# Attention with a threshold, then a feed-forward layer, on one core: preparation of the weights and of batch 0 laid out anew

## The chip, the core and the metric

The kernel runs on one core of a Trainium2 chip. A core has five engines that run side by side, each through its own queue in strict program order: TensorE (PE; its weight loads are listed as PEld), VectorE (DVE), ScalarE (ACT), GpSimd (POOL) and SyncE (SP, which here issues all transfers, run by 16 DMA engines). The metric is device time in microseconds (us) of one execution, compared by medians.

## The reference

```python
scores = (1 / sqrt(64)) * q @ k.T                    # 8 batches, 8 heads, 576 x 576
thresh = max(scores, axis=-1) - tau                  # tau = 0.02
scores = where(scores >= thresh, scores, -1e9)
attn = exp(scores - max(scores)); attn /= sum(attn) + 1e-9
x = (attn @ v), heads side by side                   # 4608 tokens x 512
h = x @ w_in                                         # 512 -> 2048
g = where(h >= 1, h, where(h <= -1, 0, (h + 1)**2 / 4))
out = g @ w_out                                      # 2048 -> 512, float32
```

q, k and v come in float32 with the head dimension first; w_in and w_out come in float64, as pairs of 32-bit words.

## The kernel before

**Precision.** Every large product is made of three float16 products: an operand is scaled by a power of two found from its own sums of squares and split into a float16 high part and a float16 low part (the remainder), and high x high, high x low and low x high are summed in PSUM.

**Weights (add_w, lines 424 to 541).** Each matrix is handled in 16 chunks of 128 x 512. A chunk of doubles is loaded to a staging place (SP, L449); ACT scales the high words to fix the exponent, in place (L457); DVE puts the float32 together in three bit passes, through a PSUM buffer `ph` (L463, L468, L472); PE squares it for the scale (L479). When all 16 chunks of a matrix are there the scale is known (lines 498 to 515), and each chunk is normalized on ACT (L522), rounded to its high part on ACT (L525), and its low part is the difference, on POOL (L528). w_in is staged in the eight places that w_out (`WO`) will need later; w_out is staged in two of the `x` buffers (`x3`, `x4`), so at most two of its chunks are under way.

**Queries, keys, values.** Two heads make a pair. add_qk loads a pair's q and k (L295), sums squares (L301, L309), makes scales on small `pc` tiles (L237 to L239 on DVE, L320 to L329 on POOL), normalizes (L337), splits (L340, L344) and copies by DMA into `qq` and `kk` (L355, L357). add_v does the same for v, and turns it by DMA transpose (L404, L409, L412).

**Attention.** The work comes in tiles of 128 queries of one head; j counts them, 288 in all (nine for each pair of a batch). A tile: four matmuls into one of two `s` buffers (L619), maximum on DVE (L630, L631, L632), exp on ACT (L635), mask and sum on DVE (L639, L643, L644), division on POOL (L647), high part on ACT (L650), low part on POOL (L653), DMA transpose into `eT` (L656). A batch's queries come in two parts, 256 of each of the four pairs and then 320; after each part PE multiplies by v (L693) into a `ph` buffer, and ACT and DVE write the two halves of `x` (L701, L705).

**Feed-forward.** A step takes 128 tokens and four chunks of 128 of the 2048: 48 matmuls (FFN1, L754) into `ph`, the gate on ACT and DVE (L760 to L775) into one of four `g` buffers, 12 matmuls (FFN2, L781) into the one `acc` bank. 144 steps. FFN1 needs all pairs of its tokens and the low parts of w_in; FFN2 the low parts of w_out.

**Order.** Nothing is scheduled by the compiler: class Plan (lines 40 to 148) walks through all operations with rough costs, and each engine takes the ready operation with the smallest key whose buffers are free; that fixes each queue's order. Keys are tile numbers. Feed-forward steps have their own key, `kf`: it starts `LEAD` = 8 tiles behind the tokens' last tile and rises by 2 for each step; FFN2 has `kf + 1`. There are three `ph` buffers, and they serve bit passes, statistics, attention x v and FFN1.

## Time and profile before

| | us |
|---|---|
| median of three runs | 1217.39 (1214.46 to 1219.19) |
| profiled execution, its own time | 1215.47 |
| its span, first to last instruction | 1213.2 |
| busy: PE, PEld | 1081.5, 788.4 |
| busy: DVE, ACT, POOL | 961.9, 885.1, 819.6 |
| DMA queue q1 | 74.7% of 16 engines' span |

The page has the span in 40 slices with a digit for the busy share of each engine in each slice; groups of instructions by line, with busy time, mean duration, and the idle time of the engine ahead of them; and other views give the same for a stretch of the span, or the instructions in order of time. A row of a timeline starts with its start and its length in us; `x12` means twelve instructions in one row. Means of short DVE instructions overlap with their neighbours, so that a sum of means is more than the busy time.

### The profile page before, as it was taken

How to read it: one execution, taken by the hardware profiler on the slowest of the kernel's cores; microseconds unless marked ns; L12 is line 12 of the kernel's file. 1: busy time of each engine (PE TensorE's matmuls, PEld its weight loads, DVE VectorE, ACT ScalarE, POOL GpSimd, SP SyncE). 2: the span in 40 equal slices, each digit the busy share in tenths (PEclk: the TensorE clock that was granted, in tenths of full speed). 3: DMA queues.
4: the chain of work that ended last, by engine and by line, in shares of the span. 5: the costliest groups of instructions: out<-in, count | busy, mean ns of one | idle time of the engine just before them, and what ended most of it. 6: DMA issues, size and time to landing. Idle time of an engine off the chain costs nothing.

```text
span 1213.2 us, 31983 instructions
## 1 busy us (share of the span) xinstructions
PE 1081.5 (89%) x11946; PEld 788.4 (65%) x11946; DVE 961.9 (79%) x2789; ACT 885.1 (73%) x1526; POOL 819.6 (68%) x939
## 2 busy tenths in 40 slices
PE   2334687999989999999999998999999999999998
...
DVE  6978987779877897788877898888877997887422
...
PEclk9956798999989999999999999999999999999999
...
GB/s 317 241 230 206 209 168 89 210 96 129 170 200 149 99 135 182 211 127 94 174 205 159 100 156 205 208 100 96 188 204 147 105 170 183 142 98 97 59 11 18
DMA packets 443818, 184.54 MB, mean 152 GB/s; under 512 B 406288, under 2 KB 414480, under 8 KB 443664
## 3 DMA queue, kind: packets, MB, share of 16 engines
q1 hardware_dynamic: 443664, 182.52, 74.7%
...
## 4 chain that ended last, share of the span: by engine, by line
PE 56%; DVE 19%; POOL 7%; ACT 7%; issue 5%; DMA 5%; SPq 1%; ACTq 0%; DVEq 0%; POOLq 0%
PE acc L781 22%; PE ph L754 21%; PE s L619 7%; PE ph L693 6%; DVE e L639 4%; DVE sm L630 4%; POOL hl L653 2%; POOL e L647 2%; DMA eT<-hl 2%; ACT e L635 1%; POOL nat L344 1%; DMA kk<-nat 1%; DVE ph L468 1%; DVE vb L409 1%; DVE ph L463 1%
## 5 line engine op out<-in xcount | busy, mean ns | idle before, releaser
L653 POOL TENSOR_TENSOR hl<-e,hl 128x576 f16<-128x576 f32 x288 | 368.0, 1283 | 98.8 <-ACT hl L650 96.4
L754 PE MATMUL ph<-x,WI 128*128 128x128 f16 x6912 | 409.3, 220 | 7.6 <-DVE x L705 4.6
L754 PEld LDWEIGHTS <-WI 128*128 128x128 f16 x6912 | 398.5, 98 | 22.1 <-issue 10.4
L781 PE MATMUL acc<-WO,g 128*128 128x512 f16 x1728 | 399.5, 382 | 4.6 <-DVE g L775 3.9
L647 POOL TENSOR_SCALAR e<-e,sm 128x576 f32<-128x576 f32 x288 | 218.7, 765 | 163.1 <-DVE sm L643 86.0
L781 PEld LDWEIGHTS <-g 128*128 128x128 f16 x1728 | 165.5, 98 | 195.3 <-DVE g L775 10.7
L635 ACT ACTIVATE e<-s,sm,pc 128x576 f32<-128x576 f32 x288 | 236.4, 828 | 69.7 <-DVE sm L631 56.9
L630 DVE TENSOR_REDUCE sm<-s 128x1 f32<-128x576 f32 x288 | 216.1, 751 | 65.5 <-PE s L619 62.3
L639 DVE SCALAR_TENSOR_TENSOR e<-s,sm,e 128x576 f32<-128x576 f32 x288 | 230.4, 813 | 30.4 <-ACT e L635 23.6
L650 ACT ACTIVATE hl<-e 128x576 f16<-128x576 f32 x288 | 194.7, 680 | 74.9 <-POOL e L647 68.6
L619 PE MATMUL s<-kk,qq 128*128 128x288 f16 (+1 forms) x1280 | 187.7, 298 | 51.2 <-DVE e L639 45.1
L619 PEld LDWEIGHTS <-qq 128*128 128x128 f16 (+1 forms) x1280 | 111.4, 103 | 103.2 <-issue 69.0
L767 DVE SCALAR_TENSOR_TENSOR ph<-ph,scs,asq 128x512 f32<-128x512 f32 (+1 forms) x160 | 111.6, 700 | 62.0 <-ACT asq L763 60.3
L760 ACT ACTIVATE asq<-ph,scs 128x512 f32<-128x512 f32 (+1 forms) x160 | 115.3, 731 | 51.5 <-PE ph L754 50.7
L693 PE MATMUL ph<-eT,vst 128*64 128x256 f16 (+1 forms) x1792 | 127.8, 295 | 8.2 <-DVE g L775 4.0
L775 DVE SCALAR_TENSOR_TENSOR g<-ph,scs,g 128x512 f16<-128x512 f32 (+1 forms) x160 | 109.0, 689 | 28.6 <-ACT g L771 28.2
L693 PEld LDWEIGHTS <-vst 128*64 128x64 f16 x1792 | 100.9, 113 | 32.5 <-issue 17.5
L771 ACT ACTIVATE g<-ph,scs 128x512 f16<-128x512 f32 (+1 forms) x160 | 100.8, 641 | 28.5 <-DVE ph L767 26.5
L763 ACT ACTIVATE asq<-asq 128x512 f32<-128x512 f32 x144 | 90.4, 628 | 1.7
L344 POOL TENSOR_TENSOR nat<-raw,nat 128x576 f16<-128x576 f32 x64 | 81.6, 1280 | 8.7 <-ACT nat L340 8.2
L631 DVE TENSOR_SCALAR sm<-sm,pc 128x1 f32<-128x1 f32 x288 | 61.7, 214 | 10.4
L340 ACT ACTIVATE nat<-raw 128x576 f16<-128x576 f32 x64 | 43.2, 679 | 34.5 <-POOL raw L337 27.2
...
## 6 DMA issues: line engine op xcount, KB each, us to landing
kk<-nat SPq DMA_DIRECT2D x128, 144.0 KB, 3.1
...
qq<-nat SPq DMA_DIRECT2D x128, 72.0 KB, 2.3
...
```

The source lines that it names most:

```text
L619: T.matmul(ap(s, s_ps)[r, f, :SH], q[:, hd, c : c + n], k[:, hd, l, f * SH : (f + 1) * SH], start=l == 0, stop=l == 1)
L630: V.tensor_reduce(t[:, 0:1], sv(), AX.XY, ALU.max, negate=True)
L635: A.activation(halves(ap(e, es)), sv(), AF.Exp, bias=ap(m, sm)[:, 1:2], scale=ap(cb, pc)[:, 24 + v, 0:1])
L639: V.scalar_tensor_tensor(halves(ap(e, es)), sv(), t[:, 2:3], halves(ap(e, es)), ALU.is_ge, ALU.mult, accum_out=t[:, 3:4])
L647: G.tensor_scalar(ap(e, es), ap(e, es), ap(m, sm)[:, 5:6], 1.0, ALU.mult, ALU.mult)
L650: A.activation(ap(x, hl)[:, :S], ap(e, es), AF.Copy)
L653: G.tensor_tensor(ap(x, hl)[:, S:], ap(e, es), ap(x, hl)[:, :S], ALU.subtract)
L693: T.matmul(o[hd * D : (hd + 1) * D, :n], vt[:, k, hd * D : (hd + 1) * D], t[:, kb, hd * n : (hd + 1) * n], start=k == 0, stop=k == NVB - 1)
L754: T.matmul(h[:, i], WTh["i"][:, u, wl * 512 + c * P : wl * 512 + (c + 1) * P], x[:, cc, xl, c0 : c0 + P], start=m == 0, stop=m == 3 * NCC - 1)
L760: A.activation(tv()[:, :, c], hv()[:, :, c], AF.Relu, bias=scs[:, b, 2:3], scale=scs[:, b, 1:2])
L767: V.scalar_tensor_tensor(hv()[:, :, c], hv()[:, :, c], scs[:, b, 0:1], tv()[:, :, c], ALU.max, ALU.min)
L781: T.matmul(ap(ab, accs), gv()[:, i, gl], WTh["o"][:, fc + i, wl * 512 : (wl + 1) * 512], start=fc + i == 0 and m == 0, stop=fc + i == NFC ...
```

## The change

- **Weights' bit passes.** DVE's first pass (L463) goes. ACT, in place of the exponent fix, converts the low words to their top bits straight into `ph` (new line 530); the fix moves to POOL (line 523); DVE keeps two passes (535, 539).
- **Weights' low parts.** For all 16 chunks of w_in and every other chunk of w_out, POOL makes the high part with the scale in one instruction (606), PE makes the low part in PSUM: a float32 matmul with a diagonal of the scale, minus the high part (609, 610), and ACT writes it to float16 (613). The other eight chunks of w_out go as before.
- **Staging of w_out.** Nine places in place of two: four `x` buffers, the output buffer, and four places of `WO` that are free by then. Only `x0` is open for attention's results until w_out is in.
- **Batch 0.** Its queries come in parts of 128, 128 and 320, so that the first eight tiles are 128 queries of all heads. FFN1 of 128 tokens waits only for those tokens. These eight tiles skip POOL, and the DMA: PE turns and divides them by a float32 matmul with a diagonal (757), ACT and DVE write the two parts (766, 769). v of batch 0 is turned on PE the same way (469, 472, 476). The rest of batch 0 has 10 blocks to turn where there were 9, and 15 products with v where there were 14.
- **Scales.** The `pc` scale passes write PSUM where they wrote strided SBUF, with a copy more (line 349).
- **Keys.** matmuls of a tile get the key j - 12, attention x v its key - 6, `LEAD` is 14 (4 for the first group), the step 1.8, FFN2 `kf + 6`; preparation has new keys.

```diff
+WOFF = 2
+NPT = 8
+KQ, KV = (-5.9, -2.7, 0.5, 3.7), -2.1
+KI, KO = (-5.8, 0.73), (8.6, 0.3)
+QKP, AVP = 12, 6
+LEAD0, LEAD = 4, 14
+KF, F2 = 1.8, 6
...
-            def b1(stage=stage, pb=pb):
+            def low(stage=stage, pb=pb):
                 if F64:
-                    V.tensor_scalar(ap(pb, ph).bitcast(U32), stage()[:, :, 1], 3, None, ALU.logical_shift_left)
+                    A.activation(ap(pb, ph).bitcast(U32), stage()[:, :, 0], AF.Copy, scale=0.935 * 2.0 ** -29)
...
-                    V.scalar_tensor_tensor(t, stage()[:, :, 0], 29, t, ALU.logical_shift_right, ALU.bitwise_or)
+                    V.scalar_tensor_tensor(t, stage()[:, :, 1], 3, t, ALU.logical_shift_left, ALU.bitwise_or)
...
-                    A.activation(t, t, AF.Copy, scale=2.0 ** -112)
+                    G.tensor_scalar(t, t, 2.0 ** -112, 1.0, ALU.mult, ALU.mult)
...
+            def split(src=src, hi=hi):
+                G.tensor_scalar(hi, src, s[:, 0:1], 1.0, ALU.mult, ALU.mult)
+            def diff(src=src, hi=hi, lb=lb):
+                T.matmul(ap(lb, ph), dgw[w], src, start=True, stop=False)
+                T.matmul(ap(lb, ph), minus, hi, start=False, stop=True)
+            def rest(lo=lo, lb=lb):
+                A.activation(lo, ap(lb, ph), AF.Copy)
...
+        d_op = plan.op("POOL", 0.25, j, lambda: G.tensor_scalar(ap(d, dge), ident, ap(m, sm)[:, 5:6], 1.0, ALU.mult, ALU.mult), [o, c_op], take=[d], uses=[m])
+        for k0, k1 in ((0, 4), (4, 5)):
...
+                    T.matmul(ap(tb, ph)[:, (k - k0) * P : (k - k0 + 1) * P], ap(e, es)[:, k * P : (k + 1) * P], ap(d, dge), start=True, stop=True)
...
-        o = chained("qk", plan.op("PE", 0.5 if len(heads) == 1 else 0.7, j, qk, ready, take=[s], uses=[qb, kb], behind=prev.get("qk")))
+        o = chained("qk", plan.op("PE", 0.5 if len(heads) == 1 else 0.7, j - QKP, qk, ready, take=[s], uses=[qb, kb], behind=prev.get("qk")))
...
-            o = chained("f2", plan.op("PE", 12 * 0.216, kf + 1.0, ffn2, [o] + wo, take=[ab] if fc == 0 else [], uses=[qb, ab], behind=prev.get("f2")))
+            o = chained("f2", plan.op("PE", 12 * 0.216, kf + F2, ffn2, [o] + wo, take=[ab] if fc == 0 else [], uses=[qb, ab], behind=prev.get("f2")))
-            kf += 2.0
+            kf += KF
```

What this makes of the queues, at three places. On DVE, in the kernel before, around the last chunks of w_in (`ph` is the PSUM buffer that a chunk is put together in, `WO` the staging place, `sm` and `e` belong to a tile):

```order
L472 SCALAR_TENSOR_TENSOR WI_67<-WO_68,ph1_64 128x512
L463 TENSOR_SCALAR ph2_65<-WO_68 128x512
L463 TENSOR_SCALAR ph0_63<-WO_68 128x512
L468 SCALAR_TENSOR_TENSOR ph2_65<-WO_68,ph2_65 128x512
L237 TENSOR_SCALAR pc1_114<-ph1_64 128x6
L238 TENSOR_SCALAR pc1_114<-pc1_114 128x6
L239 TENSOR_SCALAR pc1_114<-pc1_114 128x6
L639 SCALAR_TENSOR_TENSOR e2_93,sm2_121<-s0_61,sm2_121,e2_93 128x576
L472 SCALAR_TENSOR_TENSOR WI_67<-WO_68,ph2_65 128x512
```

and in the changed kernel, around the last three chunks of w_in:

```order
L769 TENSOR_TENSOR eT1_99<-ph0_63,eT1_99 128x128
L535 SCALAR_TENSOR_TENSOR ph2_65<-WO_68,ph2_65 128x512
L717 TENSOR_SCALAR sm4_122<-sm4_122 128x1
L718 RECIPROCAL sm4_122<-sm4_122 128x1
L539 SCALAR_TENSOR_TENSOR WI_67<-WO_68,ph2_65 128x512
L535 SCALAR_TENSOR_TENSOR ph1_64<-WO_68,ph1_64 128x512
L713 SCALAR_TENSOR_TENSOR e1_92,sm5_123<-s1_62,sm5_123,e1_92 128x576
L809 SCALAR_TENSOR_TENSOR x0_103<-ph0_63,x0_103 128x128
L539 SCALAR_TENSOR_TENSOR WI_67<-WO_68,ph1_64 128x512
```

A chunk has two rows where it had three, and what is between them are rows of a tile that is turned on PE (L769 writes the low part of `eT`) and already a row of x (L809).

Where w_in's parts are made: on ACT, in the kernel before, right after its scale (`wsc_i`) is known:

```order
L522 ACTIVATE WI_67<-WI_67,wsc_i_135 128x512 x2
L525 ACTIVATE WI_67<-WI_67 128x512 x2
L301 ACTIVATE junk_127,pc3_116<-raw6_75 128x576
L522 ACTIVATE WI_67<-WI_67,wsc_i_135 128x512
L301 ACTIVATE junk_127,pc3_116<-raw0_69 128x576
L635 ACTIVATE e0_91<-s0_61,sm0_119,pc2_115 128x576
L525 ACTIVATE WI_67<-WI_67 128x512
```

and on POOL, in the changed kernel, at the same point:

```order
L585 TENSOR_SCALAR dgw_i_130<-ident_128,wsc_i_141 128x128
L606 TENSOR_SCALAR WI_67<-WI_67,wsc_i_141 128x512 x2
L750 TENSOR_SCALAR dge1_134<-ident_128,sm7_125 128x128
L523 TENSOR_SCALAR WO_68<-WO_68 128x512 x2
L606 TENSOR_SCALAR WI_67<-WI_67,wsc_i_141 128x512
L523 TENSOR_SCALAR WO_68<-WO_68 128x512
L721 TENSOR_SCALAR e0_91<-e0_91,sm0_118 128x576
L606 TENSOR_SCALAR WI_67<-WI_67,wsc_i_141 128x512
```

The two rows on ACT became one on POOL (L606), which shares its queue with the exponent fixes of w_out (L523) and the first tiles' divisions (L721).

On PE, in the changed kernel, the place where FFN1 first stands (`dgw` is the diagonal of the scale, `vst` v turned, `x0` the first 256 tokens' x):

```order
L797 MATMUL ph2_65<-eT0_98,vst2_89 64x128
L609 MATMUL ph0_63<-WI_67,dgw_i_130 128x512
L610 LDWEIGHTS minus_129
L610 MATMUL ph0_63<-WI_67,minus_129 128x512
L864 LDWEIGHTS WI_67
L864 MATMUL ph1_64<-x0_103,WI_67 128x128
```

The 16th and last difference of w_in (L609, L610) stands right ahead of the first FFN1 (L864). Up to that row PE has 80 matmuls of tiles (L693), where the kernel before has 92; up to the end of the eighth FFN2 both have 176.

More of the change, by code (lines that the diff above doesn't have):

```diff
@@ L7 @@
 from concourse._compat import with_exitstack
+from concourse.masks import make_identity
 F16 = mybir.dt.float16
@@ L266, in attn_ffn_kernel @@
     for b in range(B):
-        parts += [(b, p, h) for h in range(2) for p in range(NPAIR)]
+        parts += [(b, p, q0, n) for q0, n in (CUT0 if not b else CUT) for p in range(NPAIR)]
     tiles = []
     first, last = {}, {}
-    for i, (b, p, h) in enumerate(parts):
+    for i, (b, p, q0, n) in enumerate(parts):
         first[i] = len(tiles)
-        n, q0 = (S1, S0) if h else (S0, 0)
         r = n % P
@@ L280, in attn_ffn_kernel @@
     NS = len(tiles)
-    start = {x: first[i] for i, x in enumerate(parts)}
-    pidx = {x: i for i, x in enumerate(parts)}
+    start = {}
+    for i, (b, p, q0, n) in enumerate(parts):
+        start.setdefault((b, p), first[i])
     QK = {}
@@ L479, in gram @@
                     T.matmul(ap(gbuf, accs)[:, :P], c, c, start=u == 0 and x == 0, stop=u == NU - 1 and x == 3)
-            before = []
-            if w == "o":
-                before = [wbits["i", x] for x in range(NU) if x % (NFC // 2) == (u + 2) // 2]
-            l = plan.op("SP", 0.6, key - 5, load, before, take=[sb], work=1.75)
-            o1 = plan.op("ACT", 0.6, key - 1, fix, [l], uses=[sb])
-            o2 = plan.op("DVE", 0.55, key, b1, [o1] + before, take=[pb], uses=[sb])
-            o3 = plan.op("DVE", 0.62, key, b2, [o2], uses=[sb, pb])
-            o4 = wbits[w, u] = plan.op("DVE", 0.62, key, b3, [o3], uses=[sb, pb], behind=wbits.get((w, u - 1)))
+            mine = (at, at + 1) if isinstance(at, int) else (at,)
+            before = [x for n in mine for x in staged.get(n, [])]
+            over = list(staged.get(u + WOFF, [])) if w == "o" else []
+            l = plan.op("SP", 0.6, key - 5, load, before, work=1.75)
+            o1 = plan.op("POOL", 0.75, key - 1, fix, [l])
+            o2 = plan.op("ACT", 0.6, key, low, [l], take=[pb])
+            o3 = plan.op("DVE", 0.62, key, b2, [o1, o2], uses=[pb])
+            o4 = wbits[w, u] = plan.op("DVE", 0.62, key, b3, [o3] + over, uses=[pb], behind=wbits.get((w, u - 1)))
+            for n in mine:
+                staged[n] = [o4]
+            if w == "o" and u in XGIVE:
+                o4.gives = ("x", XGIVE[u])
             if not u:
@@ L532, in add_w @@
-                wlo[w, u] = plan.op("POOL", 1.15, key2, rest, [o])
-            else:
-                def split(src=src, hi=hi):
-                    A.activation(hi, src, AF.Copy, scale=s[:, 0:1])
-                def rest(src=src, hi=hi, lo=lo):
-                    V.scalar_tensor_tensor(lo, src, s[:, 0:1], hi, ALU.mult, ALU.subtract)
-                o = plan.op("ACT", 0.65, key2, split, before)
-                wlo[w, u] = plan.op("DVE", 0.9, key2, rest, [o])
+                o = plan.op("ACT", 0.57, key2, norm, [so])
@@ L543, in attn_ffn_kernel @@
+            def rest(lo=lo, lb=lb):
+                A.activation(lo, ap(lb, ph), AF.Copy)
+            o = plan.op("POOL", 0.75, key2, split, [wdf.get((w, u - WOFF)), so])
+            o = wdf[w, u] = plan.op("PE", 1.1, key2, diff, [o, dg], take=[lb])
+            wlo[w, u] = plan.op("ACT", 0.52, key2, rest, [o], uses=[lb])
     wbits = {}
-    def w_pool(w, u):
-        return True
     for b in range(B):
         for p in range(NPAIR):
-            t0 = start[b, p, 0]
-            add_qk(b, p, t0 if (b, p) != (0, 0) else -20)
-        add_v(b, start[b, 0, 0] + (0 if b else 4))
@@ L662, in add_tile @@
         o = plan.op("DVE", 0.26, j, sden, [o], uses=[m])
-        o = chained("norm", plan.op("POOL", 0.77, j, snorm, [o], uses=[e, m], behind=prev.get("norm")))
-        o = chained("hi", plan.op("ACT", 0.58, j, shi, [o], take=[x], uses=[e], behind=prev.get("hi")))
-        o = plan.op("POOL", 1.26, j, slo, [o], uses=[e, x])
-        o = chained("tr", plan.op("SP", 1.3, j, send, [o], take=[eTb[i]] if j == first[i] else [], uses=[x, eTb[i]], work=1.7, behind=prev.get("tr")))
-        part_tr[i].append(o)
+        take = [eTb[i]] if j == first[i] else []
```

221 lines of the change are left out of this document (149 added, 72 removed).

## The prediction

> **What bounds the kernel now.** I read the page's slices first: where is PE, the engine with the most work, not full?
>
> ```profile
> PE   2334687999989999999999998999999999999998
> DVE  6978987779877897788877898888877997887422
> PEclk9956798999989999999999999999999999999999
> ```
>
> PE is full from about the eighth slice (30.3 us each) to the end. Ahead of that it is a third to two thirds busy, DVE is at 7 to 9 tenths, and PE's granted clock is down to about half in slices 3 to 5. So there are two stages: a preparation that PE doesn't set, and a long stage that PE does. For where the one ends I took PE's timeline:
>
> ```profile
> 10.24 0.61 PE L479 MATMUL acc<-WI 128*128 128x128 bf16 x4 [3.45 <-DVE WI L472]
> 130.38 0.40 PE L479 MATMUL acc<-WO 128*128 128x128 bf16 x4
> 132.54 2.84 PE L754 MATMUL ph<-x,WI 128*128 128x128 f16 x48 [1.71 <-DVE x L705]
> 177.41 2.75 PE L781 MATMUL acc<-WO,g 128*128 128x512 f16 x12
> 200.13 4.95 PE L781 MATMUL acc<-WO,g 128*128 128x512 f16 x12
> 211.13 2.09 PE L693 MATMUL ph<-eT,vst 128*64 128x320 f16 x28
> 213.15 5.35 PE L781 MATMUL acc<-WO,g 128*128 128x512 f16 x24
> ```
>
> FFN1 starts at 132.5, FFN2 at 177.4, and the eighth FFN2 ends at 213.15 + 5.35 = 218.5. That last point is my milestone, since at the end of the eighth FFN2 both orders have done 176 matmuls of tiles and eight FFN1; the changed one is one product with v (2.09 us) short. Whatever the change gains up to there is kept if PE stays full behind it. A step costs PE 2.84 and 2.75 where the clock is full, and an FFN2 4.95 where it isn't; four matmuls of 128 columns took 0.61 early and 0.40 later, the same difference. Then the windows, cut at first FFN1 and at the milestone (us busy of PE, PEld, DVE, ACT, POOL; clock; DMA share; GB/s):
>
> ```profile
> 0.00:132.50 132.50, 49.73 (x337) 30.96 (x338) 109.38 (x293) 88.07 (x159) 88.81 (x117) 0.77 0.99 250
> 132.50:218.50 86.00, 69.68 (x701) 50.13 (x701) 68.16 (x193) 68.30 (x122) 74.64 (x81) 0.90 0.76 144
> 218.50:1213.20 994.70, 962.11 (x10911) 707.29 (x10908) 784.37 (x2304) 728.69 (x1247) 656.13 (x743) 0.99 0.72 140
> ```
>
> Up to 218.5 the sums are PE 119.4, DVE 177.5, ACT 156.4, POOL 163.5, and DMA 0.99 x 132.5 + 0.76 x 86 = 196.5. DVE, with 0.81 of the time, is the most loaded engine; the DMA engines are as loaded, but part of what they carry is the next batch, which nobody waits for yet. Behind the milestone PE idles 994.7 - 962.1 = 32.6 us.
>
> **The change, part by part.** First the preparation; the rows that price it:
>
> ```profile
> L463 DVE TENSOR_SCALAR ph<-x 128x512 uint32<-128x512 uint32 x16 | 11.1, 691 | 5.4 <-ACT x L457 5.3
> L457 ACT ACTIVATE x<-x 128x512 f32<-128x512 f32 x16 | 10.6, 661 | 3.1 <-DMA x<-in_moe_w_out_dram 3.0
> L522 ACT ACTIVATE WO<-WO,wsc_o 128x512 f32<-128x512 f32 x16 | 11.0, 721 | 0.0
> L525 ACT ACTIVATE WO<-WO 128x512 f16<-128x512 f32 x16 | 9.5, 629 | 0.0
> L528 POOL TENSOR_TENSOR WO<-WO 128x512 f16<-128x512 f32 x16 | 18.3, 1158 | 1.2 <-ACT WO L525 1.2
> L647 POOL TENSOR_SCALAR e<-e,sm 128x576 f32<-128x576 f32 x288 | 218.7, 765 | 163.1 <-DVE sm L643 86.0 <-DVE sm L644 70.5 <-DVE pc L237 5.6
> L653 POOL TENSOR_TENSOR hl<-e,hl 128x576 f16<-128x576 f32 x288 | 368.0, 1283 | 98.8 <-ACT hl L650 96.4
> L650 ACT ACTIVATE hl<-e 128x576 f16<-128x576 f32 x288 | 194.7, 680 | 74.9 <-POOL e L647 68.6 <-DMA eT<-hl 5.4
> L404 POOL TENSOR_SCALAR vb<-raw,scs 128x1152 f16<-128x1152 f32 x32 | 39.2, 1225 | 15.0 <-DVE scs L396 14.3 <-DVE sm L643 0.4 <-DMA vst<-vb 0.2
> L409 DVE SCALAR_TENSOR_TENSOR vb<-raw,scs,vb 128x576 f16<-128x576 f32 x32 | 37.2, 1161 | 5.3 <-POOL vb L404 5.3
> ```
>
> ```profile
> L771 ACT ACTIVATE g<-ph,scs 128x512 f16<-128x512 f32 x128 | 87.4, 684 | 25.0 <-DVE ph L767 23.1 <-PE acc L781 0.9
> L775 DVE SCALAR_TENSOR_TENSOR g<-ph,scs,g 128x512 f16<-128x512 f32 x128 | 95.1, 743 | 23.8 <-ACT g L771 23.3
> L705 DVE SCALAR_TENSOR_TENSOR x<-ph,x 128x256 f16<-128x256 f32 x64 | 26.6, 416 | 8.8 <-ACT x L701 8.7
> ```
>
> *DVE.* The first bit pass goes: 32 x 0.691 = -22.1. Four subtractions for v go (4 x 1.161 = -4.6). Twelve turned pieces (four of v, eight tiles) each need a subtraction of 512 columns from PSUM, 0.743 as L775, and one of 128, for which I take 0.28 (between 0.214 for 64 columns on the same line and L705's 0.416 for 256; the trace has no 128): +12.3. x in eight parts of 128 for four of 256: +0.6. Sum -13.8: 163.7.
>
> *POOL.* 24 of 32 subtractions go: 24 x 1.158 = -27.8. The first eight tiles skip POOL: 8 x (0.765 + 1.283) = -16.4; v of batch 0: 4 x 1.225 = -4.9. Added: 32 exponent fixes and 24 scaled high parts, each at L647's rate for 512 columns, 0.765 x 512/576 = 0.68: +38.1 (the trace has neither on POOL; the bounds are 0.54 by L404, 1.06 ns a column, and 1.14 by L653: +30 to +64). Eleven diagonals and 17 clears at about 0.2: +5. Sum -6: 157.5 (150 to 184).
>
> *ACT.* 24 normalizations and high parts go: 24 x (0.721 + 0.629) = -32.4. The exponent fix (0.661) becomes the conversion of low words, of the same size, at the same price; it hides where the fix hid. 24 low parts come from PSUM at L771's 0.684: +16.4. Eight high parts of tiles go (8 x 0.680 = -5.4), twelve turned pieces come (0.684 + 0.28): +11.6, x +0.6. Sum -9.2: 147.2.
>
> *PE.* New are 60 turned blocks of 128 columns and 24 differences of 512, all float32 but the second half of each difference. No row shows float32 on PE. Lower end, as float16 at full clock (2.84/48 = 0.059, 2.75/12 = 0.229): 60 x 0.059 + 48 x 0.229 = 14.5. Upper end: this kernel itself cuts an operand into two pieces, two by two make four products; four at the slow rows (0.61/4, 4.95/12): 60 x 0.61 + 24 x 5 x 0.413 = 86. I take four products at the full clock, 60 x 0.236 + 24 x 5 x 0.229 = 42, because they fill gaps that now let the clock fall. PE: 161 (134 to 205). The Trainium skill (FP8 and Floating Point Precision, TensorE Precision Notes) gives true float32 four passes through the array; by it the sum is the 42 where the clock is full and the 86 where it isn't.
>
> *DMA.* Twelve transposes leave the front of SP's queue and the DMA engines; the other 20 of batch 0 have 10 blocks for 9.
>
> ```profile
> q1 hardware_dynamic: 443664, 182.52, 74.7%
> ```
>
> That is 906 us for 182.5 MB; eight tiles of 0.295 MB and four v of 0.459 are 4.2 MB, -21, and the longer ones +3: about 179 is left. Every row behind them on SP, loads of w_out among them, is issued earlier by as much. Loads of w_out no longer wait for two places, so POOL and DVE can take up w_out while w_in is split.
>
> So up to the milestone the most loaded are DMA 179, DVE 164, PE 161, POOL 158. It was DVE with 0.81. Now four are near each other, and a chunk goes through POOL, PE and ACT in turn, which costs share; against it DVE, which everything else stood behind, is relieved. I take 0.83 for DVE: milestone at 198, 20.5 us earlier. Bounds: 0.90 (182), and 0.75, which POOL had (218, no gain). First FFN1, by DVE's work ahead of it (21 bit passes of two instructions for 29 of three, 16 tiles for 21, so some 73 us at 0.7): 104.
>
> Then the long stage. Who PE waited for there (us, times, longest):
>
> ```profile
> PE s L619 <- DVE e L639: 10.8, 13, 4.2
> PE ph L693 <- DVE g L775: 4.0, 4, 2.3
> PE acc L781 <- DVE g L775: 3.9, 7, 1.3
> PE ph L693 <- DVE pc L237: 2.7, 1, 2.7
> ```
>
> The waits of FFN2 for g (3.9) go: with `kf + 6` and steps of 1.8 two or three other steps lie between. Of the waits for DVE's mask (10.8) and for `ph` buffers (4.0, 2.7) I take half off, since tiles are ordered up to 12 ahead and DVE is relieved by the scale passes:
>
> ```profile
> L238 DVE TENSOR_SCALAR pc<-pc 128x6 uint32<-128x6 uint32 x32 | 17.5, 545 | 1.1
> L239 DVE TENSOR_SCALAR pc<-pc 128x6 uint32<-128x6 uint32 x32 | 17.1, 534 | 1.1
> L238 DVE TENSOR_SCALAR scs<-scs 128x1 uint32<-128x1 uint32 x8 | 1.2, 154 | 0.3
> ```
>
> Two passes at 0.54 become three that I price by the 0.154 of the same pass on `scs`: 0.62 for each of 32 pairs, 20 us of DVE, 2.5 a batch, none of it on PE. Together -11 (0 to -27, all that was waited for; below, a wait more, is the last rival). FFN1's and FFN2's own work is unchanged and hides nothing new.
>
> Sum: 1213.2 - 20.5 + 2.1 (the product with v) - 11 = 1183.8; with 2.3 around the span 1186; the median stood 1.9 above the profiled execution, so **1188**.
>
> **The rivals.** *PE sets the preparation.* All float32 at the upper end: 205 us on PE, at 0.93 the milestone is at 220, and 1213.2 + 1.5 + 2.1 - 11 + 4.2 = 1210. For it: bursts before ran at half speed. Against it: the clock was 0.99 wherever PE was full. The Trainium skill (TensorE: Matmul & The Clock Gate, Part 1) has the clock at half after an idle window of some 3.4 us and full after a busy one; by that rule the added work keeps it up and this rival fails. The row of the first window, 0.77 with PE busy 0.38 of it, agrees in direction.
>
> *The start is gained and lost again on `ph`.* Three buffers now serve bit passes (from ACT's conversion on, earlier than before), turned pieces and differences too. The waits of attention x v for `ph` above show the ring short already. If it holds shares to 0.75, the milestone stays at 218 and the steady gain is used up by batch 0's extra products: 1217.
>
> *All of it works better:* milestone at 182, all waits gone: 1213.2 - 36.5 + 2.1 - 27 + 4.2 = 1156.
>
> *Slower: tiles ahead of steps make PE stand.* PE's queue is strict, and a tile's first matmul waits for DVE's mask two tiles before. Before, 13 of some 276 did, 10.8 us in all. With keys 12 ahead each tile stands in front of a step that could run. At 0.17 us a tile on the mean, 47 us, it gives 1188 + 47 = 1235; slower than no change from 0.13 on, (1223.5 - 1188)/276. Against it: tiles stand singly between steps of 2.8 us, so there are 5 us between two of one buffer.
>
> **The numbers.** Less than 0.5% (6 us) can't be told from no change here. Forecast (1168 to 1204) 0.61; better 0.13; PE sets the start 0.10; lost again 0.08; slower 0.08. The range, 1160 to 1211, leaves out half of the better case and most of the last two. Faster: 0.61 + 0.13 + 0.06 (half or so of the case at 1210) = 0.80; same 0.04 + 0.08 = 0.12; slower 0.08.
>
> **What would show it.** First FFN1 near 104 and the eighth FFN2's end near 198 in PE's timeline; DVE some 14 us less up to there; a float32 difference of 1.1 us for both halves (0.46 and 2.1 are the ends); a clock over 0.77 in the first 100 us; PE's idle time behind the milestone near 22 us. I am wrong if PE is full ahead of the first FFN1, if `ph` releases the longest waits there, or if tiles' matmuls wait more than 11 us in the long stage.

## The result, and the profile of the changed kernel

The changed kernel takes 1170.91 us (median of four runs, 1169.09 to 1174.35), the one before 1215.93 (1214.04 to 1219.19, four runs): the ratio is 0.963, with a 95% interval of 0.9595 to 0.9666, that is 45 us less. The profiled execution took 1169.14 us, its span is 1167.4. The forecast was 1188 in a range of 1160 to 1211: direction and range were right, the gain was some 17 us larger than forecast.

The slices of the changed kernel's page, each now 29.2 us:

```profile
PE   4687889999999999999999999999999999999998
DVE  5899888889888998889888888888778998884232
PEclk9799899999999999999999999999999999999999
```

In slices 2 to 5 PE is 6 to 8 tenths busy, where it was 3 to 6, and it is full from the seventh slice on. The clock's digits 5, 6 and 7 of the old slices 3 to 5 have become 9, 9 and 8; slice 2 shows a 7 where it had a 9. PE's timeline of the changed kernel, with a few rows of the new float32 work (each float32 matmul is recorded as two MATMUL, so `x8` is four blocks) and the milestones:

```profile
14.36 2.08 PE L469 MATMUL ph<-dgv,raw 128*128 128x128 f32 x8 [1.48 <-POOL dgv L460]
24.81 1.16 PE L469 MATMUL ph<-dgv,raw 128*128 128x128 f32 x8 [0.97 <-DVE vst L476]
102.08 1.02 PE L609 MATMUL ph<-WI,dgw_i 128*128 128x512 f32 x2
102.94 0.38 PE L610 MATMUL ph<-WI,minus 128*128 128x512 f16 x1
106.00 1.13 PE L609 MATMUL ph<-WI,dgw_i 128*128 128x512 f32 x2
106.96 0.38 PE L610 MATMUL ph<-WI,minus 128*128 128x512 f16 x1
107.64 2.84 PE L864 MATMUL ph<-x,WI 128*128 128x128 f16 x48 [0.30 <-DVE WO L539]
140.03 2.75 PE L891 MATMUL acc<-WO,g 128*128 128x512 f16 x12
187.79 5.34 PE L891 MATMUL acc<-WO,g 128*128 128x512 f16 x24
```

FFN1 starts at 107.6 (132.5 before), FFN2 at 140.0 (177.4), and the eighth FFN2 ends at 187.79 + 5.34 = 193.1 (218.5).

The clock shown for the first microseconds is too high, in both kernels. Four float32 blocks take 2.08 us at 14.36 and 1.16 at 24.81, and the profile grants 1.00 in both places; the rows run at half speed up to 20.4. In the kernel before it shows 1.00 for the first 52 us, too, and its rows there are slow: four matmuls of a tile take 1.12, as in the row below, and 0.65 in the changed kernel at 127.43.

```profile
51.60 1.12 PE L619 MATMUL s<-kk,qq 128*128 128x288 f16 x4 [0.35 <-DVE e L639]
```

With half the clock in these stretches the mean ahead of the first FFN1 would be some 0.57 in the kernel before, where the profile has 0.77, and some 0.80 in the changed one, where it has 0.90 (estimates from these rows).

The windows cut at the first and the last of these (columns as in the prediction):

```profile
0.00:107.60 107.60, 71.96 (x579) 49.99 (x580) 88.14 (x261) 74.96 (x152) 78.20 (x147) 0.90 0.86 261
107.60:193.10 85.50, 75.31 (x754) 52.05 (x754) 73.50 (x215) 66.56 (x116) 73.26 (x87) 0.96 0.72 139
193.10:1167.40 974.30, 957.73 (x10944) 705.07 (x10941) 777.92 (x2339) 731.57 (x1255) 660.12 (x751) 1.00 0.76 145
```

Up to the milestone the kernel is 25.4 us shorter; behind it 20.4 us, in spite of one product with v more. There PE idles 974.3 - 957.7 = 16.6 us where it idled 32.6, and is busy 957.7 where it was 962.1. Whom PE waits for behind the milestone, by lines (the rows end with the idle time ahead of the instructions and its releasers), first in the kernel before:

```profile
L754 PE MATMUL ph<-x,WI 128*128 128x128 f16 x6528 | 382.5, 219 | 2.8 <-DVE x L705 1.5 <-DVE g L775 0.9 <-DVE pc L237 0.4
L781 PE MATMUL acc<-WO,g 128*128 128x512 f16 x1633 | 376.0, 381 | 4.4 <-DVE g L775 3.9 <-ACT g L771 0.3
L619 PE MATMUL s<-kk,qq 128*128 128x288 f16 (+1 forms) x1104 | 152.7, 288 | 11.1 <-DVE e L639 10.8
L693 PE MATMUL ph<-eT,vst 128*64 128x256 f16 (+1 forms) x1568 | 108.5, 290 | 8.2 <-DVE g L775 4.0 <-DVE pc L237 2.7 <-DVE scs L394 0.8
```

and in the changed kernel:

```profile
L864 PE MATMUL ph<-x,WI 128*128 128x128 f16 x6528 | 385.5, 219 | 2.1 <-DVE x L809 1.2 <-DVE g L885 0.8
L891 PE MATMUL acc<-WO,g 128*128 128x512 f16 x1633 | 373.7, 379 | 0.0
L693 PE MATMUL s<-kk,qq 128*128 128x288 f16 (+1 forms) x1104 | 155.9, 287 | 7.9 <-DVE e L713 5.2 <-DMA kk<-nat 2.5
L797 PE MATMUL ph<-eT,vst 128*64 128x320 f16 (+1 forms) x1598 | 108.9, 287 | 1.4 <-DMA eT<-hl 1.4
```

Products with v waited 8.2 us and now 1.4, FFN2 4.4 and now nothing, tiles 11.1 and now 7.9, 5.2 of it for the mask (L713).

### The profile page after: what moved, and what is told of

The parts are those of the page before. It is cut to its first block, busy times and chain, and to the rows that moved or that the text cites. A ratio compares the mean times of both kernels' runs of the same rounds, so it can differ in the third digit from the quotient of the medians.

```text
span 1167.4 us, 32610 instructions
## 1 busy us (share of the span) xinstructions
PE 1105.0 (95%) x12274; PEld 807.1 (69%) x12274; DVE 939.6 (80%) x2813; ACT 873.1 (75%) x1522; POOL 811.6 (70%) x983
## 3 DMA queue, kind: packets, MB, share of 16 engines
q1 hardware_dynamic: 430480, 179.24, 75.7%
## 4 chain that ended last, share of the span: by engine, by line
PE 64%; DVE 12%; POOL 8%; DMA 5%; issue 5%; ACT 4%; SPq 1%; POOLq 0%; ACTq 0%; DVEq 0%
PE ph L864 25%; PE acc L891 23%; PE s L693 8%; PE ph L797 7%; DVE sm L704 3%; DMA eT<-hl 2%; DVE e L713 2%; POOL hl L729 2%; POOL e L721 1%; POOL nat L378 1%; DMA kk<-nat 1%; DMA WO<-in_moe_w_in_dram 1%; POOL raw L371 1%; ACT hl L726 1%; DVE ph L877 1%
## 5 line engine op out<-in xcount | busy, mean ns | idle before, releaser
L729 POOL TENSOR_TENSOR hl<-e,hl 128x576 f16<-128x576 f32 x280 | 359.8, 1290 | 100.3 <-ACT hl L726 98.2
L864 PE MATMUL ph<-x,WI 128*128 128x128 f16 x6912 | 409.8, 219 | 5.1 <-DVE g L885 3.6
L864 PEld LDWEIGHTS <-WI 128*128 128x128 f16 x6912 | 396.3, 98 | 21.0 <-issue 8.6
L891 PE MATMUL acc<-WO,g 128*128 128x512 f16 x1728 | 395.0, 379 | 0.0
L721 POOL TENSOR_SCALAR e<-e,sm 128x576 f32<-128x576 f32 x280 | 212.9, 764 | 99.5 <-DVE sm L718 68.0
L713 DVE SCALAR_TENSOR_TENSOR e<-s,sm,e 128x576 f32<-128x576 f32 x288 | 231.9, 812 | 34.2 <-ACT e L709 31.0
L726 ACT ACTIVATE hl<-e 128x576 f16<-128x576 f32 x280 | 189.8, 679 | 70.2 <-POOL e L721 46.9
L693 PE MATMUL s<-kk,qq 128*128 128x288 f16 (+1 forms) x1280 | 182.5, 289 | 12.8 <-DVE e L713 9.9
L693 PEld LDWEIGHTS <-qq 128*128 128x128 f16 (+1 forms) x1280 | 106.5, 100 | 69.1 <-issue 31.7
L885 DVE SCALAR_TENSOR_TENSOR g<-ph,scs,g 128x512 f16<-128x512 f32 (+1 forms) x160 | 109.1, 691 | 27.0 <-ACT g L881 26.8
L797 PE MATMUL ph<-eT,vst 128*64 128x320 f16 (+2 forms) x1928 | 126.1, 283 | 4.3 <-DVE eT L769 2.8
L705 DVE TENSOR_SCALAR sm<-sm,pc 128x1 f32<-128x1 f32 x288 | 61.7, 214 | 10.2
L706 DVE TENSOR_SCALAR sm<-sm,pc 128x1 f32<-128x1 f32 x288 | 58.8, 204 | 0.0
```

Source lines behind the costliest of these rows:

```text
L693: T.matmul(ap(s, s_ps)[r, f, :SH], q[:, hd, c : c + n], k[:, hd, l, f * SH : (f + 1) * SH], start=l == 0, stop=l == 1)
L713: V.scalar_tensor_tensor(halves(ap(e, es)[:, :S]), sv(), t[:, 2:3], halves(ap(e, es)[:, :S]), ALU.is_ge, ALU.mult, accum_out=t[:, 3:4])
L721: G.tensor_scalar(ap(e, es)[:, :S], ap(e, es)[:, :S], ap(m, sm)[:, 5:6], 1.0, ALU.mult, ALU.mult)
L726: A.activation(ap(x, hl)[:, :S], ap(e, es)[:, :S], AF.Copy)
L729: G.tensor_tensor(ap(x, hl)[:, w : w + S], ap(e, es)[:, :S], ap(x, hl)[:, :S], ALU.subtract)
L797: T.matmul(o[hd * D : (hd + 1) * D, :n], vt[:, k, hd * D : (hd + 1) * D], t[:, kb, hd * n : (hd + 1) * n], start=m == 0, stop=m == len(blo ...
```

## The experiments

Since a span is the time in which PE is busy and the time in which it isn't, one table holds all kernels (us; span, busy and idle from the profiled execution; the ratio to the kernel before, from timed runs on the same chip, with its 95% interval). "Idle behind" is PE's idle time behind the end of the eighth FFN2. That end itself can only be compared where as many tile matmuls precede it: 176 in the kernels marked *, 180 in three passes and two places, 172 with tiles off PE; in the others 124 to 200.

| kernel | time | ratio, interval | PE busy | PE idle | idle behind | end of eighth FFN2 |
|---|---|---|---|---|---|---|
| before | 1215.9 | 1 | 1081.5 | 131.7 | 32.6 | 218.5 * |
| changed | 1170.9 | 0.963, 0.9595 to 0.9666 | 1105.0 | 62.4 | 16.6 | 193.1 * |
| old keys | 1204.4 | 0.9912, 0.9879 to 0.9946 | 1120.3 | 85.6 | 40.5 | 191.5 |
| before, new keys | 1192.3 | 0.9805, 0.9776 to 0.9834 | 1075.6 | 114.8 | 16.3 | 225.0 |
| tiles not ahead | 1189.6 | 0.9787, 0.9751 to 0.9823 | 1112.7 | 72.4 | 29.4 | 182.2 |
| FFN2 near | 1194.9 | 0.9822, 0.9793 to 0.9852 | 1114.9 | 77.7 | 31.3 | 188.9 |
| tiles further ahead | 1187.2 | 0.9761, 0.9735 to 0.9787 | 1110.8 | 73.2 | 28.3 | 189.8 * |
| step 1.85 | 1166.9 | 0.9592, 0.9563 to 0.962 | 1107.5 | 58.3 | 12.5 | 195.2 * |
| old scales | 1177.4 | 0.9694, 0.9654 to 0.9734 | 1108.5 | 66.3 | 19.1 | 196.4 * |
| three passes | 1199.9 | 0.987, 0.9851 to 0.9889 | 1115.1 | 82.6 | 25.5 | 211.9 |
| low parts off PE | 1194.8 | 0.9826, 0.9808 to 0.9844 | 1094.3 | 97.8 | 34.5 | 177.6 |
| tiles off PE | 1183.7 | 0.9736, 0.9713 to 0.976 | 1102.0 | 83.4 | 30.6 | 187.0 |
| two places | 1184.3 | 0.9747, 0.9724 to 0.9769 | 1111.6 | 70.3 | 21.2 | 200.3 |
| difference twice | 1177.4 | 0.9682, 0.9657 to 0.9708 | 1120.0 | 55.4 | 15.3 | 203.3 * |

**Old keys.** The changed kernel with the keys of before for tiles, steps and FFN2; the preparation and its keys stay new.

```diff
-QKP, AVP = 12, 6
-LEAD0, LEAD = 4, 14
-KF, F2 = 1.8, 6
+QKP, AVP = 0, 0
+LEAD0, LEAD = 8, 8
+KF, F2 = 2.0, 1
```

> The changed kernel with the order's old keys (tiles' matmuls and attention x v at their own tile number, steps 8 tiles behind and 2 apart, FFN2 at kf + 1); preparation's new keys stay. Behind the eighth FFN2 the change gained 20.4 us: PE's idle time fell from 32.6 to 16.6, and 4.4 us of busy time went too. Theory A, the keys made it: PE's idle time there goes back to about 32, and the time to 1188 to 1194 (0.978 to 0.982 of the kernel before). Theory B, the scale passes made it, which take 20 us off DVE: the time stays within 4 us of 1171 (0.960 to 0.966). The eighth FFN2 ends near 193 in both.

**Before, new keys.** The other way round: the kernel before with `LEAD` 14, tiles' matmuls and products with v at j - 12 and its key - 6, the step 1.8 and FFN2 at `kf + 6`, in the five lines of its code that hold these numbers.

```diff
...
-            kf += 2.0
+            kf += KF
...
```

> The kernel before with only the new keys of the order (tiles 12 ahead, attention x v 6 ahead, steps 14 behind and 1.8 apart, FFN2 at kf + 6). Theory A, the keys make the gain of the long stage: 1194 to 1202 (0.983 to 0.989), PE's idle time behind the eighth FFN2 near 17 us. Theory B, the scale passes make it: 1212 to 1220 (0.997 to 1.003), idle near 32. First FFN1 stays at about 132 in both, as preparation is not touched.

Old keys took 1204.4, ten above the upper end of what I had expected; the new keys alone 1192.3, two below the lower end. Both say the same: the keys are worth more than my long stage gave them, 24 us on the old preparation (1216.6, the kernel before on that chip, to 1192.3) and 33 on the new (1204.4 to 1170.9). The preparation is worth 12 with old keys, 21 with new ones. The table tells the two apart: with new keys on the old preparation the first FFN1 stays at 132.6, but PE's idle time behind the milestone falls to 16.3, just what the changed kernel has; with old keys on the new preparation the first FFN1 is at 112.3, and 40.5 us are idle behind. So the start belongs to the preparation, and the long stage's idle time to the keys. The windows behind the milestone, of old keys and of the kernel before with new keys:

```profile
191.51:1205.90 1014.39, 973.87 (x11002) 713.60 (x11000) 801.91 (x2389) 749.52 (x1275) 678.77 (x778) 0.99 0.76 143
225.03:1190.40 965.37, 949.05 (x10810) 696.45 (x10807) 770.41 (x2268) 717.94 (x1230) 647.30 (x731) 1.00 0.74 142
```

On PE's whole span the preparation takes off 46 us of idle time (old keys) or 52 (new), the keys 17 (old preparation) or 23 (new). In busy time the preparation adds 39 or 29, and the keys take off 6 or 15. So each half is worth more beside the other one, by 6 us in idle and 9 in busy time of the profiled executions. In the medians it is 9 in all: the gain of the whole is 45, the two halves alone give 24 and 12. Where those 15 come from is seen in 100 us windows of old keys:

```profile
100.00:200.00 100.00, 85.78 (x820) 56.43 (x820) 68.28 (x217) 69.31 (x117) 68.17 (x80) 0.92 0.60 109
200.00:300.00 100.00, 89.19 (x1002) 65.37 (x999) 78.57 (x231) 72.39 (x124) 70.93 (x82) 0.93 0.83 156
300.00:400.00 100.00, 91.91 (x1022) 66.50 (x1020) 87.30 (x263) 79.40 (x138) 81.52 (x95) 0.97 0.96 181
```

and of the changed kernel:

```profile
100.00:200.00 100.00, 87.62 (x898) 60.56 (x899) 87.06 (x261) 78.58 (x139) 86.04 (x105) 0.97 0.76 146
200.00:300.00 100.00, 97.19 (x1166) 73.36 (x1164) 87.54 (x274) 83.03 (x142) 79.68 (x91) 1.00 0.91 174
300.00:400.00 100.00, 100.00 (x1166) 74.67 (x1165) 89.05 (x272) 81.61 (x145) 76.37 (x84) 1.00 0.90 168
```

With old keys the early start is not used: from 100 to 300 DVE is only 68 and 79% busy, PE stands an eighth of the time, and the granted clock there is 0.92 and 0.93, so that what PE does takes longer as well. Over the three windows old keys lose 8 + 7 + 3 = 18 us to the clock and the changed kernel 3; the difference is as large as the 15 us of busy time. That is where I see what the whole gains beyond its halves.

**Tiles not ahead.** Only the keys of tiles' matmuls and products with v go back.

```diff
-QKP, AVP = 12, 6
+QKP, AVP = 0, 0
```

> The changed kernel with tiles' matmuls and attention x v back at their own tile number; the steps' keys (14 behind, 1.8 apart, FFN2 at kf + 6) stay new. If it is the tiles ahead of the steps that keep DVE supplied, most of the keys' gain goes: 1180 to 1190 (0.971 to 0.979), and DVE waits for tiles' matmuls as long as before (54 us behind the eighth FFN2, 36 in the changed kernel). If it is the steps' lag and FFN2's distance: 1169 to 1176 (0.961 to 0.967).

It took 1189.6, within the first range: in this order 19 us hang on the tiles being ahead. PE's waits for the mask behind the eighth FFN2 rose from 5.2 to 18.8 us (us in total, times, longest):

```profile
PE s L693 <- DVE e L713: 18.8, 13, 3.6
```

The other sign that I expected, DVE waiting for tiles' matmuls as long as before, was not there (22.6 us; 36.1 in the changed kernel, 54.4 before): DVE starves less in the long stage, and more at the hand-over, where it is busy 45.8 of the 74.7 us between the first FFN1 and the eighth FFN2.

**FFN2 near.** Only FFN2 goes back to one key behind its step.

```diff
-KF, F2 = 1.8, 6
+KF, F2 = 1.8, 1
```

> The changed kernel with FFN2 one key behind its step, as before, in place of six; steps, tiles and preparation stay. Theory A (my forecast: FFN2's distance is worth only the waits for g that it removes, 3.9 us): 1173 to 1178, and FFN2 waits for g some 4 us. Theory B (the distance is a good part of the long stage's gain, since one step less in between also keeps tiles from their turn): 1180 to 1192.

It took 1194.9, above even the second range. Taken out alone, this one number loses 24 us, and I had given it 3.9. PE's waits behind the eighth FFN2 in this kernel (us in total, times, longest):

```profile
PE s L693 <- DVE e L713: 14.7, 9, 5.4
PE ph L864 <- DVE pc L349: 5.8, 2, 3.2
PE acc L891 <- DVE g L885: 1.3, 3, 0.9
PE acc L891 <- ACT g L881: 0.5, 1, 0.5
```

FFN2's own waits are only 1.3 for DVE and 0.5 for ACT; the loss shows at tiles (14.7 us, longest 5.4) and at FFN1 (5.8, for a `ph` buffer in which scales are made). In PE's queue FFN1 stands 2.7 steps ahead of its FFN2 in the changed kernel, on the mean of steps 21 to 110, and 1.0 here (1.1 in the kernel before). So the distance is a reserve for the whole queue: with it a late gate delays nothing, and without it the queue, planned tight, is late at whatever comes next. That the reserve is what does it is my reading of these rows; the runs show its size, not each link. Nor is 24 its share of the gain: with the 19 of the tiles it makes 43, where all keys together lose 33 on this preparation.

**Tiles further ahead.**

```diff
-QKP, AVP = 12, 6
+QKP, AVP = 18, 9
```

> The changed kernel with the tiles' matmuls 18 tiles ahead in place of 12, and attention x v 9 in place of 6. Theory A (the order ahead pays because PE always has a tile ready, and is limited by the two buffers of scores, not by the key): the gain is used up at 12, 1166 to 1178, PE idle behind the milestone 13 to 22. Theory B (the rival on tiles ahead of steps: the strict queue makes PE stand for the mask): 1180 to 1200, and PE waits more than 11 us for the mask there.

It took 1187.2, as the rival has it. Whom PE waited for behind the milestone in this kernel (us in total, times, longest):

```profile
PE s L693 <- DVE e L713: 17.4, 16, 3.9
PE ph L864 <- DVE x L809: 2.0, 3, 0.9
```

and its window from 200 to 300 us:

```profile
200.00:300.00 100.00, 88.30 (x972) 64.21 (x971) 84.00 (x259) 77.27 (x135) 80.49 (x101) 0.93 0.92 184
```

The waits for the mask are 17.4 us, above the 11 that I had named, and with them comes a clock of 0.93. The loss that the slower rival named exists at 18 tiles, and at 12 the change stays short of it. But the mark that I set for it, more than 11 us of waits for the mask, doesn't tell its mechanism from others: tiles not ahead have 18.8 us of them, and FFN2 near has 14.7. Tiles not ahead at all and tiles 18 ahead both lose 16 to 19 us.

**Step 1.85.** The smallest change of an order.

```diff
-KF, F2 = 1.8, 6
+KF, F2 = 1.85, 6
```

> The changed kernel with the step key 1.85 in place of 1.8, the smallest change of the order: it asks how much of the gain is the chance of one order. Theory A (the gain is a mechanism that any order of this kind has): 1165 to 1178. Theory B (this order is a lucky one among its neighbours): 1180 to 1192, most of it as PE idle time in 100 to 400 us.

It took 1166.9, 4 us below the changed kernel, with overlapping intervals: not told apart from it, and the gain isn't one lucky order's, as a neighbouring order has it too. Against the kernel before it is the fastest run here (0.9592). Differences of 4 us between orders are best not given a cause.

**Old scales.** The `pc` passes go back to strided SBUF.

```diff
...
-            c, t = ap(cb, pc), ph[sb.slot]
-            pow2(t[:, :6], t[:, 8:14], t[:, 16:22], c[:, 14:20])
-            V.tensor_scalar(c[:, 8:14], t[:, 16:22], 1.0, None, ALU.mult)
+            c = ap(cb, pc)
+            pow2(stat(sb.slot, 6), c[:, 2:8], c[:, 8:14], c[:, 14:20])
```

> The changed kernel with the scale passes of q and k as before, in SBUF with a stride of two words and without the copy (rows of 30 words to make room; the diagonal for v shares its tile with that of w_out). Theory B, these passes made the gain of the long stage: 1185 to 1192 (0.975 to 0.980). Theory A, the keys made it: 1170 to 1176 (0.962 to 0.967), with the second and third pass back at 0.3 to 0.5 us each and PE's idle time behind the eighth FFN2 within 4 us of 16.6.

It took 1177.4, 1.4 above the one range and 7.6 below the other; the intervals of the two kernels still touch. The passes in it:

```profile
L262 DVE TENSOR_SCALAR pc<-pc 128x6 uint32<-128x6 uint32 x32 | 13.5, 422 | 1.1
L263 DVE TENSOR_SCALAR pc<-pc 128x6 uint32<-128x6 uint32 x32 | 10.2, 318 | 1.1
```

They take 0.422 and 0.318, less than the 0.545 and 0.534 of the kernel before, and more than the change's own (0.164, in a row further down). DVE is busy 949.1 us, 9.5 more than in the changed kernel. Of the 7.4 us of span 3.3 lie ahead of the milestone and 4.1 behind it. So the scales are worth some 6 us, a small part, and not clear of the 4 us by which two neighbouring orders differ.

**Three passes.** The bit passes as before: the fix on ACT, three passes on DVE.

```diff
-                    G.tensor_scalar(t, t, 2.0 ** -112, 1.0, ALU.mult, ALU.mult)
+                    A.activation(t, t, AF.Copy, scale=2.0 ** -112)
...
-                    A.activation(ap(pb, ph).bitcast(U32), stage()[:, :, 0], AF.Copy, scale=0.935 * 2.0 ** -29)
+                    V.tensor_scalar(ap(pb, ph).bitcast(U32), stage()[:, :, 1], 3, None, ALU.logical_shift_left)
...
```

> The changed kernel with the weights' bit passes as before: exponent fix on ACT, three passes on DVE, nothing of them on POOL. Theory A, preparation ends when the most loaded engines have done their shares: DVE has 22 us more up to the eighth FFN2, so that end moves from 193 to 208 to 218, and the time to 1186 to 1196 (0.975 to 0.983). Theory B, one chain sets it (scale of w_in, its low parts, first FFN1; then w_out's): the scale of w_in is known some 8 us later at most, and the time is 1171 to 1180 (0.963 to 0.970).

The windows of this kernel up to its first FFN1 and its eighth FFN2:

```profile
0.00:92.03 92.03, 57.37 (x410) 41.38 (x411) 76.55 (x216) 60.42 (x127) 40.84 (x95) 0.87 0.81 262
92.03:211.88 119.85, 97.36 (x925) 61.74 (x923) 102.12 (x288) 81.84 (x140) 87.38 (x99) 0.91 0.67 135
```

DVE has 76.6 + 102.1 = 178.7 us of work up to there, 17 more than the changed kernel, and the milestone is at 211.9, 18.8 later (with one tile more ahead of it). DVE's share is 0.84 in both. Here the milestone follows DVE's work almost one for one, as I had it. The time is 1199.9, 4 us over the first range, since 9 more are idle behind. The first FFN1 is at 92.0, earlier than in the changed kernel: each new plan puts it elsewhere, and it tells nothing between different orders.

**Difference twice.** PE issues the float32 half of each difference twice.

```diff
+                T.matmul(ap(lb, ph), dgw[w], src, start=True, stop=True)
                 T.matmul(ap(lb, ph), dgw[w], src, start=True, stop=False)
```

> The changed kernel, in which PE issues the first, float32 half of each of the 24 differences twice; the result is the same. It asks whether PE sets the preparation. Added are 24 x about 0.9 us = 21 us of PE ahead of or near the milestone, nothing elsewhere. Theory A (PE has room in the preparation, DVE and the transfers set it): PE idles 46 us up to the milestone of 193.1, half or more of the 21 us go there: 1171 to 1181, milestone 193 to 203. Theory B (PE, or the chain of one buffer from PE to ACT, sets it): all 21 us come on top, 1188 to 1196, milestone 210 to 216.

The windows of this kernel, cut at the same places:

```profile
0.00:115.08 115.08, 82.43 (x612) 54.53 (x613) 90.42 (x264) 76.45 (x153) 79.72 (x151) 0.93 0.83 248
115.08:203.33 88.25, 80.82 (x771) 53.04 (x770) 69.60 (x215) 68.17 (x118) 74.29 (x84) 0.98 0.73 135
203.33:1175.30 971.97, 956.71 (x10944) 704.47 (x10941) 779.81 (x2335) 729.78 (x1253) 659.55 (x749) 1.00 0.76 145
```

The milestone is at 203.3, 10.2 later, and the time 6.5 us longer, for 24 x 0.86 = 21 us of work at the full clock. PE's busy time up to the milestone rose by 16 only, with the clock at 0.93 and 0.98 in place of 0.90 and 0.96. The time is in the range of the first theory and the milestone at the end of its range, but PE's idle time up to there fell by 6 us only (45.8 to 40.1), where that theory sends half of the 21 or more. So PE doesn't set the preparation alone, but it isn't free either: half of what is added is paid at the milestone, and a third in the time, by intervals that just overlap (0.9657 against 0.9666).

**Low parts off PE** (all 32 subtractions on POOL, normalization and high part on ACT), **tiles off PE** (the first eight tiles through POOL and the DMA) and **two places** (w_out staged in `x3` and `x4`) each take one other part back.

```diff
-    return w == "i" or u % 2
+    return False
```

> The changed kernel with all low parts of the weights as before (ACT normalizes and rounds, POOL subtracts), none on PE. Theory A (shares): ACT has 16 us more and POOL 11 us more up to the eighth FFN2, PE 27 us less; POOL becomes the most loaded with about 163; 1172 to 1182 (0.964 to 0.972). Theory B (chain): w_in's 16 low parts take ACT 21 us and POOL 18.5 in a row where they took POOL 11 and PE 17 in step; first FFN1 moves from 108 to 118 or later, and the time to 1180 to 1190 (0.971 to 0.979).

```diff
-NPT = 8
+NPT = 0
```

> The changed kernel with the first eight tiles through POOL, ACT and DMA transposes as all the others (10 blocks each); v of batch 0 stays on PE. Theory A (shares): POOL has 16 us more, DVE 8 less, the DMA engines 18 us more up to the eighth FFN2: 1178 to 1190 (0.969 to 0.979). Theory B (chain): w_in's low parts set the first FFN1, not x, so little moves: 1169 to 1176 (0.961 to 0.967), first FFN1 within 4 us of 108.

```diff
...
-    OSTAGE = ["x1", "x2", "x3", "x4", "o", 10, 12, 14, 16, "x1", "x2", "x3", "x4", "o", "x1", "x2"]
+    OSTAGE = ["x3", "x4"] * 8
...
-    XGIVE = {12: [3, 4], 15: [1, 2]}
+    XGIVE = {15: [3, 4]}
```

> The changed kernel with w_out staged in two x buffers as before (the other three x buffers open to results from the start). Theory A (shares): no engine has more work, so 1170 to 1178 (0.962 to 0.969). Theory B (chain): w_out's 16 loads go two at a time behind bit passes, each round some 6 to 8 us, so that its scale is known 15 to 30 us later than at 128; the eighth FFN2 moves to 208 or later and the time to 1183 to 1196 (0.973 to 0.983).

They took 1194.8, 1183.7 and 1184.3: 24, 13 and 13 us over the changed kernel. Of the first, neither theory's time nor its place held (FFN1 came earlier, at 89.7, and the time later): PE has 11 us less to do and 35 more of idle time. The second is within the range of the theory that gives the part its due, at a DMA share of 0.97 ahead of the first FFN1 (0.86 in the changed kernel). The third has the time of the second theory, but its milestone is only 7 later, not 15. Together with three passes these four single steps lose 29 + 24 + 13 + 13 = 79 us, where the whole preparation is worth 12 to 21. So they can't be read as shares of it: each was taken out of a plan whose other numbers stay fitted to the whole, and each new plan loses in the hand-over, too. They don't show what one part is worth; if a plan only loses by a part that it isn't fitted to, each loss is an upper bound.

## Why the prediction was right, and which sizes were off

**The milestone: forecast 198, measured 193.1.** DVE's sum was 163.7 and is 88.1 + 73.5 = 161.6, its share 0.83 and is 0.84. This step held, and the run with three passes agrees: 17 us more of DVE's work move the milestone by 18.8. But DVE isn't alone in setting it. With the difference twice and with two places DVE has the same work up to there (160.0 and 160.6), and the milestone comes 10.2 and 7.2 later. POOL was forecast at 157.5 and has 151.5, ACT 147.2 and 141.5. The sum for the DMA engines was off, 179 against 0.86 x 107.6 + 0.72 x 85.5 = 154: transfers of the next batch stand later in the new order, and behind the milestone the queue carries 139.5 MB where it carried 137.2. PE waits 3.9 us for transfers there (`kk` and `eT`), where it waited 0.6. In that sum the transposes with 10 blocks are 28, not 20, which is 1.5 us more; the queue's whole load fell from 182.52 to 179.24 MB, that is by the 4.2 less 28 pieces of 0.033.

FFN1 started at 107.6, near the 104 of the forecast, and that is luck: DVE had 88.1 us of work ahead of it, not 73, at a share of 0.82, not 0.7.

The split between the two stages was off as well. The forecast had 20.5 us for the start and 11 for the long stage; undone in halves, the preparation is worth 12 to 21 and the keys 24 to 33.

**The prices.** The rows of the changed kernel for what the trace before didn't show:

```profile
L523 POOL TENSOR_SCALAR WO<-WO 128x512 f32<-128x512 f32 x20 | 12.8, 654 | 2.5 <-DMA WO<-in_moe_w_in_dram 2.3
L530 ACT ACTIVATE ph<-WO 128x512 uint32<-128x512 uint32 x20 | 12.4, 628 | 2.2 <-DMA WO<-in_moe_w_in_dram 0.8 <-DVE WI L539 0.6 <-DVE vst L476 0.4
L606 POOL TENSOR_SCALAR WI<-WI,wsc_i 128x512 f16<-128x512 f32 x16 | 11.1, 697 | 1.1 <-PE ph L609 1.1
L613 ACT ACTIVATE WI<-ph 128x512 f16<-128x512 f32 x16 | 9.5, 594 | 0.7 <-PE ph L610 0.6
L262 DVE TENSOR_SCALAR pc<-ph 128x6 uint32<-128x6 uint32 x32 | 5.3, 164 | 1.1
L769 DVE TENSOR_TENSOR eT<-ph,eT 128x512 f16<-128x512 f32 x8 | 5.5, 687 | 2.1 <-ACT eT L766 2.0
L750 POOL TENSOR_SCALAR dge<-ident,sm 128x128 f32<-128x128 f32 x8 | 3.0, 371 | 10.5 <-DVE sm L718 5.1 <-PE ph L342 2.9 <-DVE eT L769 2.5
L769 DVE TENSOR_TENSOR eT<-ph,eT 128x128 f16<-128x128 f32 x8 | 2.2, 280 | 0.0
```

The exponent fix on POOL is 0.654 (taken 0.68), the scaled high part 0.697 for w_in and 0.758 for w_out (0.68), ACT's conversion 0.628 (0.661), the low part 0.594 (0.684), turned pieces 0.687 and 0.280 (0.743 and 0.28), a diagonal 0.371 (0.2), a scale pass 0.164 (0.154). Those on POOL lie near what was taken, inside the bounds of 0.54 and 1.14.

**Float32 on PE** was taken at four float16 products: 0.236 for a block of 128 columns, 1.15 for a difference. In the timeline a float32 half starts at 106.00 and the half behind it at 106.96; others are 0.86 apart (102.08 and 102.94 in the same view), and the float16 half takes 0.21 to the next: some 1.07. Four blocks take 1.16 at 24.81, 0.29 each by the length of the row (0.22 each from start to start, in a row at 83.28), and 2.08 at 14.36, 0.52 each, where the rows run at half speed. The Trainium skill's four passes for float32 (FP8 and Floating Point Precision, TensorE Precision Notes) agree: 0.86 is 3.75 times the 0.229 of a float16 product of 512 columns. PE's sum up to the milestone is 147.3, not 161. The differences cost what I took; the turned blocks cost more, since part of them ran at half speed: their rows add up to 8.6 + 15.4 = 24.0 by length, where I took 14.2. Old work got cheaper, as the clock of the first window rose (0.77 to 0.90 in the profile): the tiles' matmuls up to the milestone, 35.2 us in the kernel before, take 26.8.

**The long stage is the step that was mis-sized: -11 forecast, -22.5 measured** (-20.4 with the product with v in it). In its idle time I took half of the waits for the mask and for `ph`, and all of FFN2's; these terms add up to 12.7, of which I put down 11. Measured are 16.0 us less: the waits for the mask were halved as forecast (10.8 to 5.2), and the products' went nearly all (8.2 to 1.4), where I took half. That is 5 of the 11.5 us. The other 6.5 are busy time (962.1 to 957.7, with 2.1 of new work in it), which my sum held unchanged. Most of that is the clock. The kernel before has a pause in the long stage, by its window from 300 to 400 us:

```profile
300.00:400.00 100.00, 92.88 (x1022) 66.95 (x1021) 80.04 (x226) 75.10 (x130) 75.30 (x92) 0.97 0.85 167
```

PE idles 7 us there and the clock is 0.97; the changed kernel has 0 and 1.00 in the same window. In rows, with a second such place:

```profile
335.53 2.08 PE L619 MATMUL s<-kk,qq 128*128 128x288 f16 x8 [4.16 <-DVE e L639]
337.40 4.58 PE L781 MATMUL acc<-WO,g 128*128 128x512 f16 x12
859.56 3.63 PE L693 MATMUL ph<-eT,vst 128*64 128x320 f16 x28 [2.75 <-DVE pc L237]
```

Around a wait of 4.16 us the granted clock is 0.50 from 334.27 to 341.10, and FFN2 takes 4.58 in place of 2.75; around one of 2.75 it is 0.50 from 859.92 to 863.34, and the product takes 3.63 in place of 2.09. These 10.2 us at half the clock are some 5 of the 6.5, and the changed kernel's clock is 1.00 in every window of 100 us behind its milestone. So a long wait costs more than its length. Not each does: behind one of 2.70 at 175.08 in the changed kernel FFN1 takes 2.85. And I gave FFN2's distance the waits that stand at FFN2, 3.9 us; taken out alone, it loses 24.

**The rivals.** PE setting the preparation fails: PE is busy 72.0 of the 107.6 us ahead of the first FFN1, and of work added to PE half is paid at the milestone. The start lost again on `ph` fails as the prediction tells it: the shares are as forecast, and ahead of the first FFN1 no wait of PE for a `ph` buffer adds up to more than 2.8 us, where those for inputs reach 6.6. Behind it the ring is still short. Two waits for a buffer that the gate holds make 5.5 of the 10.2 us for which PE idles between the first FFN1 and the milestone; the one ahead of the second FFN1, which then takes 4.35 in place of 2.84:

```profile
116.21 4.35 PE L864 MATMUL ph<-x,WI 128*128 128x128 f16 x48 [2.77 <-DVE g L885]
```

The slower one doesn't come at 12 tiles, where the waits for the mask are 5.2; its loss is there at 18. The one in which all works better came nearest in the size of the long stage (27 us, measured 22.5), though 16.6 us of idle time stayed, and it was wrong about the milestone (182).

**Still open:** what each part of the preparation and each key is worth by itself (`LEAD` was never taken back alone, nor the step to 2.0), what besides DVE sets the milestone, and by which links FFN2's distance acts on the waits of tiles.
